# A gated linear-attention start-up rearranged: own gates for the last pair of heads, the next unit's decays moved into the MLP steps, other dummies between the transposes

## The chip, the cores and the metric

One core of a Trainium2 chip runs the whole program. The metric is the device time of one execution in microseconds (us), taken as the median of several runs. Runs of one kernel on one chip lie within about 0.7 % of each other here (the kernel before: 566.09 to 569.85 us on one chip). PE is TensorE (matmuls), PEld its weight loads, DVE is VectorE, ACT is ScalarE, POOL is GpSimd, SP is SyncE, which here only issues transfers.

## The reference, cut to what matters

An attention-like recurrence, then an MLP. `B, H, S, D = 4, 8, 768, 48`, model width 384, MLP width 2048.

```python
f = 1.0 / (1.0 + np.exp(-f_logit))
for t in range(S):
    state = f[:, :, t, :, None] * state + np.einsum('bhd,bhe->bhde', k[:, :, t], v[:, :, t])
    y[:, :, t] = np.einsum('bhd,bhde->bhe', q[:, :, t], state)
x = y.transpose(0, 2, 1, 3).reshape(B * S, H * D)
h = x @ w_in
g = np.where(h > 0.0, h, np.exp(np.minimum(h, 0.0)) - 1.0)
return g @ w_out
```

The weights arrive in 64-bit floating point, and the kernel makes 32-bit ones of them while the first unit's MLP runs.

## The kernel before

The tokens are worked through in 12 units of 256. A unit holds its 8 heads as 4 pairs: pairs 0 to 2 fill most of the partitions, and the last pair (number `NKT` = 3) sits in the same layout. For each pair, `gates` makes `1 + exp(-f_logit)` on ACT, `grow` makes its running product with a scan on DVE, `fall` takes the reciprocal of that (the decay itself), and `scale` multiplies k by the product and q by the reciprocal on POOL. In the kernel before, the last pair's gates are not computed for themselves. They are spread over the spare partitions of pairs 0 to 2, and two SBUF-to-SBUF transfers per unit (`move`, written f<-f in the traces) bring the results into place.

```python
def grow(u, p):
    g = qkf[u % NB]["f"][:, p, 0]
    nc.vector.tensor_tensor_scan(out=g, data0=g, data1=g, initial=1.0, op0=ALU.mult, op1=ALU.max)
def fall(u, p):
    f = qkf[u % NB]["f"]
    nc.vector.reciprocal(f[:, p, 1], f[:, p, 0])
def move(u, which, queue):
    f = qkf[u % NB]["f"]
    for r in range(2):
        to = PAD + D * r
        queue.dma_start(out=f[to : to + D, NKT, which], in_=f[GAP[r] : GAP[r] + PAD, 0:NKT, which])
```

Each of the 16 pieces of the weights passes four stations, in this order: `fetch` (a transfer, issued by SP), `split` (two DVE operations), `lower` (one ACT operation), `merge` (one DVE operation).

```python
def split(n):
    ...
    nc.vector.tensor_scalar(out=bits[:], in0=hi, scalar1=3, scalar2=0x3FFFFFF8,
        op0=ALU.logical_shift_left, op1=ALU.bitwise_and)
    nc.vector.tensor_scalar(out=hi, in0=hi, scalar1=-(2**30), scalar2=None, op0=ALU.bitwise_and)
def lower(n):
    ...
    nc.scalar.activation(raw.bitcast(U16)[:, 2::4], raw.bitcast(U32)[:, 0::2], AF.Copy, scale=2.0**-29)
def merge(n):
    ...
    nc.vector.tensor_tensor(out=to.bitcast(I32), in0=bits, in1=hi, op=ALU.add)
    fetch(n + AHEAD)
```

The first unit's MLP runs in 16 steps, alternately `up` (x times a piece of w_in) and, two pieces behind, `down` (times a piece of w_out). Work of the second unit is hung on these steps with `at_step(step, ...)`: `advance` (state sums on PE), `step` (the same on DVE), `scores` and `mask`, `outputs`, `carried` (which finishes x of the second unit and is followed by a move xt<-xt). `warm` issues dummy matmuls. In the traces of this case an engine's work stands in the order in which the program emits it: in c1 an elu of ACT whose product PE had finished at 29.8 ran at 35.76, behind an issue of ACT's own queue, 6.01 us idle before it. So the order of the lines below is the order of each engine's work.

```python
# start of the kernel before, cut
    ...                                     # first unit: three pairs, two moves, transposes, scores 0 to 2
    a = qkf[1]["f"][:, 0:NKT, 0]            # second unit, all before the first MLP step:
    nc.vector.tensor_scalar_add(a, a, 1.0)
    for p in range(NKT):
        grow(1, p)
    move(1, 0, nc.sync)
    ...
    fall(1, 0)
    ...
    mask(0, pc)
    ...
    split(0)
    ...
    fall(1, 1)
    first_outputs(0)
    lower(0); merge(0)                      # (two lines in the source)
    first_outputs(1)
    ...
    split(1)
    transposed(1, 0, "a0"); warm(1); transposed(1, 1, "a1")
    lower(1)
    watch(0)
    fall(1, 2)
    move(1, 1, nc.scalar)
    ...
    attention(1, (), A1)                    # A1 = (2, 4, 5, 7, 8, 9): steps of the second unit's parts
    for n in range(1, NFT):                 # merge 1 and later inside the steps
        ...
```

Of the kernel before, what the change touches and what calls it, by code (L numbers as in the profile page):

```python
# [356 lines left out]
def fast(ctx: ExitStack, tc: tile.TileContext, q, k, v, f_logit, w_in, w_out, out, flag, outer):  # L357
# [38 lines left out]
    WA = 1  # L396
    W0 = 3
    HOLD = 2
    A1 = (2, 4, 5, 7, 8, 9)
# [30 lines left out]
    def load(u, names="fkqv"):  # L430
        b, s0 = u // UPB, (u % UPB) * U
        for n in names.replace("v", ""):
            to = qkf[u % NB][n][MAIN]
            frm = src[n][b, :, :, s0 : s0 + U].rearrange("(p r) d s -> (r d) p s", r=2)
            if n == "f":
                to, frm = to[:, 0:NKT, 0], frm[:, 0:NKT]
            nc.sync.dma_start(out=to, in_=frm)
            for r in range(2 if n == "f" else 0):
                nc.sync.dma_start(
                    out=qkf[u % NB][n][GAP[r] : GAP[r] + PAD, 0:NKT, 0],  # L440
                    in_=src[n][b, 2 * NKT + r, :, s0 : s0 + U].rearrange("(i j) s -> i j s", i=PAD),
                )
        if "v" in names:
            nc.sync.dma_start(
                out=vs[u % NB][:, :, PAD : PAD + DM], in_=v[b, s0 : s0 + U].rearrange("(c t) n -> t c n", t=W)
            )
# [6 lines left out]
    def blank(i, *engines, zeros=None):  # L453
# [4 lines left out]
        (zeros or engines[-1]).memset(qkf[i]["f"][:, NKT], 1.0)  # L458
# [189 lines left out]
    def watch(u):  # L648
        nc.vector.scalar_tensor_tensor(
            out=fine[:], in0=qkf[u % NB]["f"][:, 0:NKT, 0, U - 1 :], scalar=LIMIT, in1=fine[:],  # L650
            op0=ALU.is_le, op1=ALU.mult,
        )
# [378 lines left out]
    def warm(n, bank="m0"):  # L1031

        pw = ps.tile([128, 4, 128], FP32, tag=bank, name="psW")
        for _ in range(n):
            nc.tensor.matmul(
                pw[:], lhsT=ident[:], rhs=ident[:].unsqueeze(1).broadcast_to([128, 4, 128]), start=True, stop=True
            )


    gates(0, (1, 2))  # L1040
# [5 lines left out]
    for p in range(NKT):  # L1046
        grow(0, p)
        scale(0, ("k", p, nc.gpsimd))
        if p < 2:
            transposed(0, 0, "m0", (p,))  # L1050
    move(0, 0, nc.scalar)
    transposed(0, 1, "m1", (0,))
    fall(0, 0)
    scale(0, ("q", 0, nc.gpsimd))
    warm(WA, "m3")
    gates(1, bias=0)
    advance(0, (0, 1))
    pc = scores(0, ("m2", "m3"), (0,))
# [5 lines left out]
    scale(0, ("k", NKT, nc.gpsimd), ("q", 1, nc.gpsimd))  # L1064
    fall(0, 2)
    move(0, 1, nc.scalar)
    warm(4)
    transposed(0, 1, "m1", (1,))
    advance(0, (2,))
    scores(0, None, (1,), pc)  # L1070
    scale(0, ("q", 2, nc.gpsimd))
    advance(0, (3,))
    scores(0, None, (2,), pc)
    nc.gpsimd.tensor_copy(
# [3 lines left out]
    a = qkf[1]["f"][:, 0:NKT, 0]  # L1078
    nc.vector.tensor_scalar_add(a, a, 1.0)
    for p in range(NKT):  # L1080
        grow(1, p)
    move(1, 0, nc.sync)
    scale(0, ("q", NKT, nc.gpsimd))
    warm(2)
    scores(0, None, (NKT,), pc)
    warm(1)
    fall(1, 0)
    for c in range(NC - 1):
        step(0, c)
    mask(0, pc)  # L1090
    step(0, NC - 1)
    split(0)
# [10 lines left out]
    fall(1, 1)  # L1103
    first_outputs(0)
    lower(0)
    merge(0)
    first_outputs(1)
    scale(1, ("k", 0, nc.gpsimd), ("q", 0, nc.gpsimd), ("k", 1, nc.gpsimd), ("k", 2, nc.gpsimd))
    scale(1, ("k", NKT, nc.gpsimd))
    split(1)  # L1110
    transposed(1, 0, "a0")
    warm(1)
    transposed(1, 1, "a1")
    lower(1)
    watch(0)
    scale(1, ("q", 1, nc.gpsimd))
    fall(1, 2)
    scale(1, ("q", 2, nc.gpsimd))
    move(1, 1, nc.scalar)
    watch(1)  # L1120
    at_step(1, lambda: scale(1, ("q", NKT, nc.gpsimd)))
    attention(1, (), A1)
    for n in range(1, NFT):
        t = min(max(needs[n][0] - 2, 0), n)
        at_step(t, lambda n=n: merge(n))
        if n > 1:
            later.setdefault(max(t - 2, 0), []).append(n)
    at_step(8, lambda: load(2))
# [90 lines left out]
```

## Time and profile before

The time before is 568.36 us, median of 3 runs (567.65 to 569.44). Its profiled run has a span of 565.7 us on the core.

| What | Kernel before |
| --- | --- |
| first ACT exp of the first unit | 4.84 us |
| score mask starts | 20.82 us |
| first MLP step starts | 30.80 us |
| third MLP step starts | 38.79 us |
| `carried` of the second unit | 56.65 us |
| second unit's first MLP product | 76.12 us |
| span | 565.7 us |

How to read it: from about 100 us on PE is full (460.0 us busy of the 460 from 100 to 560 us; 8.63 of 10 from 90 to 100), so the row that counts is the next to last. Whatever moves the second unit's first MLP product moves the end by about as much.

Beside the lines that the prediction shows, two more of the timeline of DVE are the second unit's second and third reciprocal in the kernel before; the columns are start, duration, engine and source line, operation, tiles and shapes.

```profile
24.12 1.75 DVE L630 RECIPROCAL f<-f 128x256 f32<-128x256 f32 x1
...
29.76 1.75 DVE L630 RECIPROCAL f<-f 128x256 f32<-128x256 f32 x1
```

A reciprocal of 128x256 took 1.69 to 1.76 us in this trace (36 of them, mean 1.75), a scan of that shape 0.66 to 1.16 (mean 0.77). The columns are the stretch, its length, then PE, weight loads, DVE, ACT and POOL, each with its number of instructions, then the granted clock, the DMA share and GB/s.

```profile
10.00:20.00 10.00, 9.24 (x132) 4.72 (x130) 8.31 (x10) 2.19 (x5) 5.12 (x10) 1.00 1.08 264
...
30.00:40.00 10.00, 8.68 (x100) 6.95 (x99) 7.51 (x12) 8.60 (x9) 1.47 (x2) 1.00 0.74 179
```

DVE is idle for 1.7 us of the first of these stretches, 2.8 of the one left out and 2.5 of the last, 7.0 of 30 us; in the two stretches after them, which the prediction shows, for under 1 us of 20.

### The profile page before, as it was taken

Reading aid. Unit: us, or ns where it says so; the run is one execution under the profiler, and the core shown is the slowest. Engines: PE = TensorE matmul, PEld = TensorE weight load, DVE = VectorE, ACT = ScalarE, POOL = GpSimd, SP = SyncE. Lnnn points to the kernel's source line nnn. Section 1 sums busy time; section 2 is a strip of 40 time slices with the busy share of each in tenths; the row PEclk is TensorE's granted clock in tenths of the full one; section 3 lists DMA queues with packets and bytes.
Section 4 is the critical chain, followed back from the end, with each engine's and each line's share of the span. In section 5 each row is a group of like instructions: output and inputs, shape, how many; then the busy total and the mean of one; then the engine's idle time right before and its main releaser. Section 6 shows DMA issues by size and latency. Waiting matters only on the chain.

```text
span 565.7 us, 15532 instructions
## 1 busy us (share of the span) xinstructions
PE 548.6 (97%) x6338; PEld 510.3 (90%) x6338; DVE 408.2 (72%) x802; ACT 230.6 (41%) x424; POOL 290.9 (51%) x567
## 2 busy tenths in 40 slices
PE   6898998999999999999999999999999999999996
PEld 3576777999999999999999999999999999999995
DVE  8689889785776785785785885886786876745543
ACT  3287953334343443433433343343334344233331
POOL 6510897474374374465466357257257348325332
PEclk9999999999999999999999999999999999999999
DMA  8989871023024135225216216216206202201001
GB/s 208 262 197 287 264 161 43 3 64 99 3 56 140 53 74 138 64 53 146 79 38 158 82 38 153 86 37 155 85 22 170 85 9 72 85 2 36 30 2 35
DMA packets 38193, 53.30 MB, mean 94 GB/s; under 512 B 3712, under 2 KB 27936, under 8 KB 38112
## 3 DMA queue, kind: packets, MB, share of 16 engines
q1 hardware_dynamic: 37312, 51.62, 34.6%
q8 instruction: 52, 0.85, 0.7%
q10 hardware_dynamic: 800, 0.59, 0.4%
q14 instruction: 29, 0.24, 0.2%
HBM read 44.04 MB, written 4.72 MB: 86 GB/s over the span
## 4 chain that ended last, share of the span: by engine, by line
PE 82%; DVE 6%; ACT 4%; DMA 4%; issue 2%; POOL 1%; SPq 0%; ACTq 0%; DVEq 0%; POOLq 0%
PE psH L881 37%; PE psM L980 36%; DMA area<-in_moe_w_in_dram 2%; ACT area L572 2%; PE psS L704 2%; PE psY L742 2%; PE psY L762 2%; PE psU_a L727 2%; DVE f L630 2%; PE psT L668 1%; DMA f<-f 1%; DVE f L625 1%; DVE bits L562 1%; DMA f<-in_f_logit_dram 0%; DVE area L566 0%
## 5 line engine op out<-in xcount | busy, mean ns | idle before, releaser
L881 PE MATMUL psH<-xt,wi 128*128 128x128 f32 (+1 forms) x1056 | 194.9, 293 | 0.0
L945 POOL TENSOR_TENSOR sums<-gg 128x128 f32<-128x128 f32 x176 | 77.5, 461 | 216.3 <-DVE gg L935 204.9
L881 PEld LDWEIGHTS psH<-xt,wi 128*128 128x128 f32 x1056 | 149.5, 192 | 1.4
L913 ACT ACTIVATE gg<-hh 128x512 f32<-128x512 f32 x88 | 55.6, 632 | 231.7 <-DVE hh L903 151.6
L881 PE MATMUL psH<-xt,area 128*128 128x128 f32 x704 | 121.8, 275 | 1.4 <-DVE gg L935 0.9
L881 PEld LDWEIGHTS psH<-xt,area 128*128 128x128 f32 x704 | 106.5, 191 | 6.4 <-DVE gg L935 1.0
L890 DVE TENSOR_TENSOR hh<-psH,u 128x256 f32<-128x256 f32 x88 | 37.2, 423 | 93.8 <-ACT u L888 93.8
L980 PE MATMUL psM<-area,sums 128*128 128x192 f32 x528 | 100.3, 326 | 0.0
L980 PEld LDWEIGHTS psM<-area,sums 128*128 128x128 f32 x528 | 88.2, 190 | 0.1
L980 PE MATMUL psM<-wo,gg 128*128 128x192 f32 x352 | 74.9, 335 | 0.0
L630 DVE RECIPROCAL f<-f 128x256 f32<-128x256 f32 x36 | 62.8, 1748 | 1.1
L935 DVE SCALAR_TENSOR_TENSOR gg<-gg,hh 128x512 f32<-128x512 f32 x88 | 61.9, 703 | 1.8 <-ACT gg L914 1.8
L914 ACT ACTIVATE gg<-gg 128x512 f32<-128x512 f32 x96 | 60.7, 632 | 3.0
L980 PEld LDWEIGHTS psM<-wo,gg 128*128 128x128 f32 x352 | 55.2, 190 | 2.0
L903 DVE TENSOR_TENSOR hh<-psH,u43h 128x256 f32<-128x256 f32 (+1 forms) x176 | 54.7, 353 | 3.0
L945 POOL TENSOR_TENSOR sums<-gg,sums 128x128 f32<-128x128 f32 x88 | 47.3, 538 | 6.9
L888 ACT COPY u<-psH 128x128 f32<-128x128 f32 x88 | 23.3, 264 | 60.3 <-PE psH L881 60.3
L903 DVE TENSOR_TENSOR u43h<-psH,hh 128x256 f32<-128x256 f32 x88 | 37.2, 423 | 12.4 <-PE psH L881 11.7
L620 POOL TENSOR_TENSOR k<-k,f 128x256 f32<-128x256 f32 x48 | 39.5, 824 | 8.2 <-DMA f<-f 5.1
L980 PE MATMUL psM<-area,gg 128*128 128x192 f32 x176 | 43.0, 326 | 0.0
L980 PE MATMUL psM<-wo,sums 128*128 128x192 f32 x176 | 43.0, 326 | 0.0
L945 POOL TENSOR_TENSOR sums<-sums,gg 128x128 f32<-128x128 f32 x88 | 42.8, 487 | 0.0
(97 smaller groups left out, 665.3 us busy)
## 6 DMA issues: line engine op xcount, KB each, us to landing
area<-in_moe_w_out_dram SPq DMA_DIRECT2D x8, 768.0 KB, 8.6
again<-in_moe_w_in_dram SPq DMA_DIRECT2D x16, 384.0 KB, 4.2
again<-in_moe_w_out_dram SPq DMA_DIRECT2D x16, 384.0 KB, 3.5
k<-in_k_dram SPq DMA_DIRECT2D x12, 384.0 KB, 4.6
q<-in_q_dram SPq DMA_DIRECT2D x12, 384.0 KB, 5.6
v<-in_v_dram SPq DMA_DIRECT2D x12, 384.0 KB, 6.1
area<-in_moe_w_in_dram SPq DMA_DIRECT2D x8, 576.0 KB, 8.8
out_dram<-o SPq DMA_DIRECT2D x42, 96.0 KB, 1.7
```

Of the source, the lines that this page charges most:

```text
L572: nc.scalar.activation(raw.bitcast(U16)[:, 2::4], raw.bitcast(U32)[:, 0::2], AF.Copy, scale=2.0**-29)
L620: e.tensor_tensor(out=t[n][:, p], in0=t[n][:, p], in1=t["f"][:, p, "kq".index(n)], op=ALU.mult)
L630: nc.vector.reciprocal(f[:, p, 1], f[:, p, 0])
L881: nc.tensor.matmul(to, lhsT=lhs, rhs=rhs, start=(n == 0), stop=True, skip_group_check=True)
L888: nc.scalar.copy(u1[:], pa[:, 0])
L890: add = lambda to, x, y: nc.vector.tensor_tensor(out=to, in0=x, in1=y, op=ALU.add)
L903: add = lambda to, x, y: nc.vector.tensor_tensor(out=to, in0=x, in1=y, op=ALU.add)
L913: nc.scalar.activation(g[:], h, AF.Relu, scale=-1.0)
L914: nc.scalar.activation(g[:], g[:], AF.Exp, scale=-1.0)
L935: nc.vector.scalar_tensor_tensor(out=g[:], in0=g[:], scalar=-1.0, in1=phs.pop(P), op0=ALU.add, op1=ALU.max)
L945: nc.gpsimd.tensor_tensor(out=s[:, i], in0=x, in1=y, op=op)
L980: nc.tensor.matmul(pm[bank][:, half * DH : (half + 1) * DH], lhsT=x, rhs=y, start=first, stop=(j == NP - 1), skip_group_check=True,)
```

## The change

The intent has three parts. First, the first unit's last pair gets gates, a scan and a reciprocal of its own, so that both moves of that unit go, and with them the late scores. Second, the second unit's decays (scans, reciprocals, scaling, transposes) leave the stretch before the first MLP step, so that the first unit's own path runs through unhindered; they are hung on the first unit's MLP steps. Its outputs and `carried` come three steps later as well. Third, the dummy matmuls between the transposes get other counts and lengths. The core of the diff:

```diff
-    A1 = (2, 4, 5, 7, 8, 9)
+    F1 = (0, 1, 3)
+    A1 = (3, 6, 7, 9, 11, 12)
@@ the first unit's f: one load, filled with 50 first
+            elif n == "f":
+                to = to[:, :, 0]
+            engines[-1].memset(qkf[i]["f"][:, :, 0], 50.0)
@@ the first unit
-    gates(0, (1, 2))
+    gates(0, (1, 1, 2))
-    for p in range(NKT):
+    for p in range(HP):
         grow(0, p)
         scale(0, ("k", p, nc.gpsimd))
-    move(0, 0, nc.scalar)
+        if p:
+            warm(1, "m3", 3)
...
     fall(0, 2)
-    move(0, 1, nc.scalar)
+    fall(0, 3)
@@ the second unit, before the MLP steps
-    for p in range(NKT):
-        grow(1, p)
-    move(1, 0, nc.sync)
-    fall(1, 0)
...
-    fall(1, 1)
-    fall(1, 2)
-    move(1, 1, nc.scalar)
+    grow(1, 0)
+    grow(1, 1)
+    merge(1)
+    grow(1, 2)
+    at_step(0, lambda: move(1, 0, nc.scalar))
     watch(0)
+    watch_last(0)
@@ and inside them
+    for p in range(NKT):
+        at_step(F1[p], lambda p=p: fall(1, p), lambda p=p: scale(1, ("q", p, nc.gpsimd)))
+    at_step(F1[2], lambda: move(1, 1, nc.scalar), lambda: watch(1))
+    at_step(A1[0], lambda: transposed(1, 0, "a0"), lambda: transposed(1, 1, "a1"))
```

(The order of `split(0)`, `lower(0)`, `mask(0)` and `split(1)` ahead of the steps changes a little too; left out here.)

More of the change, by code (lines that the diff above doesn't have):

```diff
@@ L395, in fast @@
     AHEAD = 7
-    WA = 1
+    F1 = (0, 1, 3)
     W0 = 3
     HOLD = 2
-    A1 = (2, 4, 5, 7, 8, 9)
+    A1 = (3, 6, 7, 9, 11, 12)
     D2 = (16, 18, 20, 22)
@@ L434, in load @@
             frm = src[n][b, :, :, s0 : s0 + U].rearrange("(p r) d s -> (r d) p s", r=2)
-            if n == "f":
+            if n == "f" and u:
                 to, frm = to[:, 0:NKT, 0], frm[:, 0:NKT]
+            elif n == "f":
+                to = to[:, :, 0]
             nc.sync.dma_start(out=to, in_=frm)
-            for r in range(2 if n == "f" else 0):
+            for r in range(2 if n == "f" and u else 0):
                 nc.sync.dma_start(
@@ L457, in blank @@
                 e.memset(qkf[i][n][:, j * w : (j + 1) * w], 0.0)
-        (zeros or engines[-1]).memset(qkf[i]["f"][:, NKT], 1.0)
+        if i:
+            (zeros or engines[-1]).memset(qkf[i]["f"][:, NKT], 1.0)
+        else:
+            engines[-1].memset(qkf[i]["f"][:, :, 0], 50.0)
     start = ctx.enter_context(ExitStack())
@@ L650, in watch, with watch_last @@
             out=fine[:], in0=qkf[u % NB]["f"][:, 0:NKT, 0, U - 1 :], scalar=LIMIT, in1=fine[:],
+            op0=ALU.is_le, op1=ALU.mult,
+        )
+    def watch_last(u):
+        nc.vector.scalar_tensor_tensor(
+            out=fine[:, 0:1], in0=qkf[u % NB]["f"][:, NKT:, 0, U - 1 :], scalar=LIMIT, in1=fine[:, 0:1],
             op0=ALU.is_le, op1=ALU.mult,
@@ L1029, in finish_flag, with warm @@
         nc.vector.tensor_copy(flag[:], pf[0:1, :])
-    def warm(n, bank="m0"):
+    def warm(n, bank="m0", blocks=4):
         pw = ps.tile([128, 4, 128], FP32, tag=bank, name="psW")
@@ L1035, in warm @@
             nc.tensor.matmul(
-                pw[:], lhsT=ident[:], rhs=ident[:].unsqueeze(1).broadcast_to([128, 4, 128]), start=True, stop=True
+                pw[:, 0:blocks], lhsT=ident[:], rhs=ident[:].unsqueeze(1).broadcast_to([128, blocks, 128]), start=True, stop=True
             )
-    gates(0, (1, 2))
+    gates(0, (1, 1, 2))
     fetch(0)
@@ L1045, in fast @@
     warm(W0, "m3")
-    for p in range(NKT):
+    for p in range(HP):
         grow(0, p)
         scale(0, ("k", p, nc.gpsimd))
-        if p < 2:
-            transposed(0, 0, "m0", (p,))
-    move(0, 0, nc.scalar)
-    transposed(0, 1, "m1", (0,))
+        if p:
+            warm(1, "m3", 3)
+        transposed(0, p // 2, f"m{p // 2}", (p % 2,))
     fall(0, 0)
     scale(0, ("q", 0, nc.gpsimd))
-    warm(WA, "m3")
-    gates(1, bias=0)
     advance(0, (0, 1))
+    warm(1, "m3")
     pc = scores(0, ("m2", "m3"), (0,))
@@ L1063, in fast @@
     fall(0, 1)
-    scale(0, ("k", NKT, nc.gpsimd), ("q", 1, nc.gpsimd))
+    scale(0, ("q", 1, nc.gpsimd))
     fall(0, 2)
-    move(0, 1, nc.scalar)
-    warm(4)
-    transposed(0, 1, "m1", (1,))
     advance(0, (2,))
+    warm(1)
     scores(0, None, (1,), pc)
     scale(0, ("q", 2, nc.gpsimd))
+    fall(0, 3)
     advance(0, (3,))
+    warm(1)
     scores(0, None, (2,), pc)
+    scale(0, ("q", NKT, nc.gpsimd))
     nc.gpsimd.tensor_copy(
@@ L1077, in fast @@
     )
-    a = qkf[1]["f"][:, 0:NKT, 0]
-    nc.vector.tensor_scalar_add(a, a, 1.0)
-    for p in range(NKT):
-        grow(1, p)
-    move(1, 0, nc.sync)
-    scale(0, ("q", NKT, nc.gpsimd))
-    warm(2)
+    warm(1)
     scores(0, None, (NKT,), pc)
     warm(1)
-    fall(1, 0)
+    gates(1, bias=0)
     for c in range(NC - 1):
         step(0, c)
+    split(0)
+    lower(0)
     mask(0, pc)
-    step(0, NC - 1)
-    split(0)
     for c in range(NC - 1):
@@ L1102, in fast @@
         fetch(n)
-    fall(1, 1)
+    merge(0)
+    step(0, NC - 1)
     first_outputs(0)
-    lower(0)
-    merge(0)
+    split(1)
     first_outputs(1)
-    scale(1, ("k", 0, nc.gpsimd), ("q", 0, nc.gpsimd), ("k", 1, nc.gpsimd), ("k", 2, nc.gpsimd))
-    scale(1, ("k", NKT, nc.gpsimd))
-    split(1)
-    transposed(1, 0, "a0")
+    lower(1)
     warm(1)
-    transposed(1, 1, "a1")
-    lower(1)
-    watch(0)
-    scale(1, ("q", 1, nc.gpsimd))
-    fall(1, 2)
-    scale(1, ("q", 2, nc.gpsimd))
-    move(1, 1, nc.scalar)
-    watch(1)
-    at_step(1, lambda: scale(1, ("q", NKT, nc.gpsimd)))
-    attention(1, (), A1)
+    a = qkf[1]["f"][:, 0:NKT, 0]
+    nc.vector.tensor_scalar_add(a, a, 1.0)
+    grow(1, 0)
[3 more added lines that the diff above has]
+    at_step(0, lambda: move(1, 0, nc.scalar))
+    watch(0)
+    watch_last(0)
+    scale(1, ("k", 0, nc.gpsimd), ("k", 1, nc.gpsimd), ("k", 2, nc.gpsimd))
     for n in range(1, NFT):
         t = min(max(needs[n][0] - 2, 0), n)
-        at_step(t, lambda n=n: merge(n))
+        if n > 1:
+            at_step(t, lambda n=n: merge(n))
         if n > 1:
             later.setdefault(max(t - 2, 0), []).append(n)
+    for p in range(NKT):
+        at_step(F1[p], lambda p=p: fall(1, p), lambda p=p: scale(1, ("q", p, nc.gpsimd)))
+    at_step(F1[1], lambda: scale(1, ("k", NKT, nc.gpsimd)))
+    at_step(F1[2], lambda: move(1, 1, nc.scalar), lambda: watch(1))
+    at_step(F1[2] + 3, lambda: scale(1, ("q", NKT, nc.gpsimd)))
+    at_step(A1[0], lambda: transposed(1, 0, "a0"), lambda: transposed(1, 1, "a1"))
+    attention(1, (), A1)
     at_step(8, lambda: load(2))
```

## The prediction

> **What bounds the kernel now.** I read the page first (engine shares and the strip of 40 slices), then the busy time of each engine by stretches, then the chain of waits, then the timeline of the first 100 us line by line.
>
> ```profile
> PE 548.6 (97%) x6338; PEld 510.3 (90%) x6338; DVE 408.2 (72%) x802; ACT 230.6 (41%) x424; POOL 290.9 (51%) x567
> ...
> 40.00:50.00 10.00, 10.00 (x99) 7.31 (x98) 9.42 (x17) 8.11 (x7) 0.00 (x0) 1.00 1.05 287
> 50.00:60.00 10.00, 8.28 (x150) 5.93 (x149) 9.72 (x17) 8.85 (x11) 1.31 (x3) 1.00 1.05 263
> ...
> 200.00:250.00 50.00, 50.00 (x581) 48.67 (x581) 37.75 (x76) 20.25 (x42) 26.66 (x51) 1.00 0.33 88
> ```
>
> The columns after the stretch are its length, then PE, weight loads, DVE, ACT, POOL, granted clock, DMA share and GB/s. From about 100 us on PE is full to the end. So the change, which touches only the first two units, can move the end only by moving the moment at which PE becomes full. Between 40 and 60 us DVE is at 9.4 and 9.7 of 10: that stage is DVE and PE in near balance.
>
> The timeline of the start, which the change rewrites:
>
> ```profile
> 0.80 0.40 SPq L437 DMA_DIRECT2D f<-in_f_logit_dram  x1
> 1.73 0.98 POOL L458 MEMSET f<- 128x512 f32 x2
> 4.84 0.42 ACT L611 ACTIVATE f<-f 128x256 f32<-128x256 f32 x1 [2.75 <-DMA f<-in_f_logit_dram]
> 8.61 4.94 DVE L630 RECIPROCAL f<-f 128x256 f32<-128x256 f32 x3
> 15.43 1.07 POOL L620 TENSOR_TENSOR k<-k,f 128x256 f32<-128x256 f32 x1 [3.12 <-DMA f<-f]
> 18.85 0.72 POOL L620 TENSOR_TENSOR q<-q,f 128x256 f32<-128x256 f32 x1 [0.60 <-DMA f<-f]
> 20.82 1.29 DVE L712 TENSOR_TENSOR at<-psS,twice 128x512 f32<-128x512 f32 x2 [1.74 <-PE psS L704]
> 24.73 0.66 PE L807 MATMUL psY<-at,padded_v 64*32 64x64 f32 x33 [1.34 <-issue]
> 28.48 0.48 ACT L817 COPY xt<-psY 128x384 f32<-128x384 f32 x1 [0.77 <-PE psY L807]
> 30.80 2.76 PE L926 MATMUL psH<-xt,wi 128*128 128x256 f32 x12
> 33.45 0.96 DVE L580 CUSTOM_DVE_ANT_0 wi<-area,bits 128x1536 uint16<-128x1536 uint16 x1 [1.93 <-ACT area L572]
> 34.55 2.83 PE L926 MATMUL psH<-xt,wi 128*128 128x256 f32 x12 [0.99 <-DVE wi L580]
> ```
>
> The reader is to see four things. The first f load is issued at 0.80, waiting for nothing. The last pair's k and q wait for the two SBUF moves (f<-f): k at 15.43, q at 18.85. The score mask starts at 20.82, only because those scores were late. The MLP starts at 30.80, and its second step waits for a weight that DVE has to merge. After 30.80 the remaining idle of PE, up to the point where it is full, is small: 1.0 at 33.6, 0.3 at 38.5, 1.35 at 50.7, 0.3 at 52.3, 0.8 at 77.2, 0.5 at 93.4, 0.9 at 96.3, about 5.2 us in all. With the start itself this is all there is to win.
>
> [...]PE is mostly idle from 22.8 to 25.9, and the stretches 26 to 30 show granted clocks 0.66, 0.50, 0.50, 0.63. [...]
>
> **The change part by part.**
>
> (1) First load of f: one transfer of 384 KB in place of 288 and two of 48 KB, but the whole of f is first filled with 50 by POOL. That memset is POOL's third, from 1.73; 1024 elements at the row's 0.49 per 512 are 0.98, so it ends at 2.71 and the load is issued at 2.75 instead of 0.80. I take 3.6 us to landing (288 KB took 3.3; all 384 KB took 3.9 with the gaps apart): 6.35. ACT starts at 6.45 against 4.84, so **1.6 later**.
>
> (2) Gates in pieces 1, 1, 2. Exp and +1 of 0.42 each, 0.6 for two pairs: scans can start at 7.35, 8.1, 9.35, 10.1 and end at 10.9. DVE then makes four reciprocals of 1.65 (a fourth scan and a fourth reciprocal are new work, 2.4 us): 17.5. POOL's last q product 0.72, then scores 0.45: 18.75, against 20.69 before (20.23 plus 0.46). Removed: both moves, 5.1 and 5.4 us from issue to use. The PE queue with its short dummies (0.65 for three blocks, 0.86 for four, from 0.43 a record) is ready at 18.2, so it does not bind. **Net 1.9 earlier.**
>
> (3) DVE then makes two state sums and the first weight split (1.15, now ahead of the mask): mask from 19.4 to 20.7, against 20.82 to 22.1. **1.4 earlier.** From mask end to x written took 22.1 to 29.94 in the old trace (3.3 first outputs with the 1.34 gap, 0.4, 2.6, 1.46); taken over unchanged, x is there at 28.5. The second unit's transposes and dummies, which held PE until 30.80, are out of the way. So the MLP starts at 28.6: **2.2 earlier.**
>
> (4) What was paid for it. The second unit's three scans, one addition and three reciprocals were done before the MLP in DVE time in which little waited for it. Now the third scan and reciprocals stand between weight merges. ACT's lowering of weight 1 comes behind the x copies: 28.5 to 30.5, DVE having nothing from about 26.2 on, some 4 us of idle. Merge 1: 30.5 to 31.5. Then scan 0.6, watch 0.25, reciprocal 1.7, split 1.15, reciprocal 1.7, split 1.15: 38.05, then the elu 0.65 and merge 2 (0.98): 39.65. Before, merge 2 ended at 38.65. So the third MLP step starts at 39.7 against 38.79: the 2.2 are gone, **0.9 lost** instead.
>
> (5) The rest of the first unit. DVE needs per step a merge 0.98, a split 1.15 and half an elu 0.33: 2.46. PE needs 2.59 (step starts 65.78, 68.37, 70.95, 73.54). DVE therefore catches up only 0.13 a step, and has the third reciprocal (1.75), sums (2.1) and mask (1.2) on top. PE has advance, scores, outputs and carried (1.15, 1.16, 1.5, 1.35). Following both queues in program order: up2 39.7, down0 42.3, up3 46.35 (waits for merge 4), down1 49.0, up4 51.6, scores 54.2, down2 55.35, up5 58.25 (merge 8), outputs 61.6 (mask), down3 63.0, carried 65.6, up6 66.95, down4, up7, down5 at 69.55, 72.15, 74.75, and the second unit at 77.3. Before: 76.12. **1.2 later.**
>
> (6) The second unit's x comes out three steps later (step 12 instead of 9). Carried ends at 66.95, ACT copies after its pending lowering 69.6 to 71.5, the move took 6.0 before: 77.5, and POOL's blend needs three of its five operations (3.79 for five, so 2.3) for the second product. If the move is as slow again, **0 to 2.3 more**; the blend had 3 us to spare before (done at 73.34).
>
> The sum: plus 1.2 to plus 3.5, less what (3) may be better than I took it.
>
> **The rivals.** First, the early gain survives: if the 1.34 us instruction gap and the half clock (36 small products in 1.17 and 1.49 us) do not recur, x is 1 to 2 us earlier still, merge 1 with it, and DVE's debt is cancelled: minus 1 to minus 2.5, 566 to 567.5. For it: the step numbers look tuned to the new order. Against: DVE was full from 37.5 to 62.5 and gets 2.4 us more work. Second, DVE becomes the bound of the first unit's steps, as worked out: 569.5. Third, x of the second unit arrives too late, POOL is held at the blend, and as it is 8 to 9 tenths busy from 60 to 100 us its backlog delays the sums too: 571 to 573. Fourth, PE idles from about 35 to 39.7 and drops to half clock: 1.3 to 2.6 more in the third step, but hidden where DVE binds.
>
> **Range and chances.** Second and third rival are plus 1.2 to plus 4, the first minus 1 to minus 2.5; I give the first 4 in 10, as small timing shifts decide it. Weighted: about plus 0.6. Predicted 569.0 us against 568.36, range 565.5 to 572.5. Two per cent is 11.4 us, more than the 5.2 us of idle plus the start shift could give, so faster 0.02, within 0.95, slower 0.03.
>
> **What would show it.** (1) f issue near 2.75 and first ACT exp near 6.4. (2) no f<-f on the first unit; last scores near 18.7. (3) first MLP product at 28 to 29. (4) DVE idle of some 4 us before merge 1, and the third MLP step at 39 to 40 waiting for DVE. (5) the second unit's first product at 77 or later, DVE over 9 tenths from 31 to 62. (6) a wait of PE or POOL for xt<-xt near 77. It is wrong if the second unit starts before 75.5, if ACT starts its exp before 5.5, or if PE shows new gaps after 100 us.

## The result, and the profile after

| | before | after |
| --- | --- | --- |
| time, median (same rounds, 4 runs each) | 568.66 us | 572.16 us |
| range | 567.65 to 569.44 | 571.24 to 572.57 |
| first ACT exp | 4.84 | 6.66 |
| last scores of the first unit | 20.23 | 19.81 |
| score mask starts | 20.82 | 20.39 |
| first MLP step starts | 30.80 | 27.13 |
| third MLP step starts | 38.79 | 39.37 |
| `carried` of the second unit | 56.65 | 67.90 |
| second unit's first MLP product | 76.12 | 79.62 |
| span of the profiled run | 565.7 | 569.4 |

The result is correct. The ratio is 1.0060, 95 % interval 1.0039 to 1.0082. Here and below a ratio is the mean time of one kernel's fast runs over that of the other's of the same rounds, so it is not quite the ratio of the medians quoted. The changed kernel is 0.6 % slower, inside 2 % and inside the predicted range, but at its upper end: 3.5 us lost where 0.6 was predicted. (On the chip of the experiments below the same kernel loses 4.9 to 5.1 us by its ratio of 1.0087.)

The line numbers in the trace after are 5 to 11 higher than before; it is the same code. The start, from the timeline of ACT, DVE and PE of the changed kernel:

```profile
6.66 0.42 ACT L616 ACTIVATE f<-f 128x256 f32<-128x256 f32 x1 [4.57 <-DMA f<-in_f_logit_dram]
11.26 6.56 DVE L635 RECIPROCAL f<-f 128x256 f32<-128x256 f32 x4
20.39 1.29 DVE L723 TENSOR_TENSOR at<-psS,twice 128x512 f32<-128x512 f32 x2 [0.63 <-PE psS L715]
27.13 2.86 PE L937 MATMUL psH<-xt,wi 128*128 128x256 f32 x12 [0.49 <-ACT xt L830]
29.07 0.96 DVE L585 CUSTOM_DVE_ANT_0 wi<-area,bits 128x1536 uint16<-128x1536 uint16 x1 [1.73 <-ACT area L577]
```

The reader is to see that the intent came true. The first step starts 3.67 us earlier than before, the second step 4.37 us earlier (30.18 against 34.55). Then it is lost. The same view, from DVE's and PE's timeline, for the next ten microseconds:

```profile
30.72 0.73 DVE L660 SCALAR_TENSOR_TENSOR fine<-f,fine 128x1 f32<-128x1 f32 x1
31.38 1.74 DVE L635 RECIPROCAL f<-f 128x256 f32<-128x256 f32 x1
...
33.56 0.96 DVE L571 TENSOR_SCALAR area<-area 128x768 int32<-128x768 int32 x1
34.44 1.74 DVE L635 RECIPROCAL f<-f 128x256 f32<-128x256 f32 x1
...
38.10 1.12 DVE L585 CUSTOM_DVE_ANT_0 wi<-area,bits 128x1536 uint16<-128x1536 uint16 x1
...
41.20 1.75 DVE L635 RECIPROCAL f<-f 128x256 f32<-128x256 f32 x1
...
38.46 0.69 PE L679 MATMUL psT<-ident,k 128*128 128x128 f32 x2 [4.80 <-POOL k L625]
39.37 5.37 PE L937 MATMUL psH<-xt,wi 128*128 128x256 f32 x12 [0.22 <-DVE wi L585]
```

Two reciprocals stand between merge 1 (29.07) and merge 2 (38.10), and a third follows at 41.20. PE meanwhile waits 4.80 us for the last pair of the second unit's k, which waits for a move, and when it has that, the third step's weight is only just merged. Two chains, one over DVE and one over the move and POOL, end within a microsecond of each other, at 39.2 and 38.4. And the third step itself takes 5.37 us against 2.83: PE runs at half clock (granted clock 0.50 from 38 to 44 us). The stretches, with the granted clock third from the end:

```profile
30.00:40.00 10.00, 4.80 (x22) 3.78 (x23) 9.83 (x14) 5.50 (x5) 3.28 (x4) 0.88 0.78 199
40.00:50.00 10.00, 10.00 (x92) 7.48 (x91) 9.65 (x14) 8.17 (x9) 0.98 (x1) 0.77 0.90 242
...
60.00:70.00 10.00, 8.79 (x153) 6.51 (x152) 9.83 (x14) 8.23 (x8) 9.06 (x13) 1.00 1.05 322
```

From 30 to 70 us DVE is at 9.3 to 9.8 of 10 (9.32 in the stretch left out), and PE has 5.2 us of idle in the first of these stretches alone. Before, PE was at 8.68 there. The last loss comes at the end of the second unit's attention, from the timeline of ACT and PE:

```profile
65.89 1.94 ACT L577 ACTIVATE area<-area 128x768 uint16<-128x768 uint32 x1
67.57 0.47 ACT L760 COPY between<-psY 128x8 f32<-128x8 f32 x2
...
67.90 1.35 PE L773 MATMUL psY<-q,state 64*64 64x64 f32 x64 [1.21 <-ACT between L760]
...
79.62 0.38 PE L892 MATMUL psH<-xt,wi 128*128 128x128 f32 x2
```

PE waits for two small copies of ACT, which stand in ACT's queue behind a weight's lowering, and that waits for DVE's split, which ended at 65.9. After 79.62 the two traces run side by side to the end, 3.5 us apart at the start and 3.7 at the end.

### The profile page after: what moved, and what is told of

Its sections match the earlier page's. It is cut to its first block, busy times and chain, and to the rows that moved or that the text cites. A ratio compares the mean times of both kernels' runs of the same rounds, so it can differ in the third digit from the quotient of the medians.

```text
span 569.4 us, 15523 instructions
## 1 busy us (share of the span) xinstructions
PE 549.0 (96%) x6338; PEld 510.0 (90%) x6338; DVE 413.3 (73%) x805; ACT 231.0 (41%) x426; POOL 294.1 (52%) x567
## 4 chain that ended last, share of the span: by engine, by line
PE 83%; DVE 5%; ACT 3%; DMA 2%; issue 1%; POOL 1%; ACTq 0%; SPq 0%; DVEq 0%
PE psH L892 37%; PE psM L991 36%; ACT area L577 2%; PE psS L715 2%; PE psY L753 2%; PE psY L773 2%; PE psU_a L738 2%; DMA area<-in_moe_w_in_dram 2%; PE psT L679 1%; DVE f L635 1%; PE psM L969 1%; DVE bits L567 1%; DVE wi L585 1%; DVE wo L585 1%; DVE gg L946 1%
## 5 line engine op out<-in xcount | busy, mean ns | idle before, releaser
L635 DVE RECIPROCAL f<-f 128x256 f32<-128x256 f32 x37 | 64.4, 1746 | 1.1
L625 POOL TENSOR_TENSOR q<-q,f 128x256 f32<-128x256 f32 x48 | 36.4, 758 | 18.1 <-DMA f<-f 6.8
```

What stands on the lines that cost most here:

```text
L625: e.tensor_tensor(out=t[n][:, p], in0=t[n][:, p], in1=t["f"][:, p, "kq".index(n)], op=ALU.mult)
```

## The experiments

All twelve but one give the reference's result; that one is wrong. The times of before that the ratios of the twelve use are of the same chip (567.2 to 567.4 us; 568.66 for the result itself, on another chip). This table has what each run's profile says of the two points that matter. The profile is of one execution: the same kernel gave 79.62 (after) and 80.60 (after_again), so differences of under 1 us in its columns are not resolved.

| run | second unit's first product | span | span less product | median | ratio to before (95 %) |
| --- | --- | --- | --- | --- | --- |
| before | 76.12 | 565.7 | 489.6 | 568.36 | |
| after | 79.62 | 569.4 | 489.8 | 572.16 | 1.0060 (1.0039 to 1.0082) |
| k1_keep_clock | 80.14 | 570.5 | 490.4 | 572.30 | 1.0089 (1.0062 to 1.0116) |
| k2_cheap_recip (wrong result) | 77.55 | 567.0 | 489.5 | 569.92 | 1.0050 (1.0022 to 1.0078) |
| k3_first_only | 88.51 | 577.7 | 489.2 | 580.26 | 1.0232 (1.0204 to 1.0261) |
| k4_second_only | 80.82 | 570.8 | 490.0 | 572.41 | 1.0085 (1.0057 to 1.0113) |
| after_again | 80.60 | 570.7 | 490.1 | 572.35 | 1.0087 (1.0066 to 1.0107) |
| k3b_first_only | 77.41 | 566.9 | 489.5 | 568.54 | 1.0026 (0.9999 to 1.0052) |
| r3_early | 81.15 | 570.4 | 489.3 | 571.88 | 1.0087 (1.0059 to 1.0114) |
| r4_early_pool | 81.85 | 570.1 | 488.3 | 573.49 | 1.0109 (1.0080 to 1.0139) |
| c1_order | 79.12 | 568.6 | 489.5 | 571.09 | 1.0078 (1.0056 to 1.0100) |
| c2_all | 77.41 | 567.2 | 489.8 | 569.53 | 1.0042 (1.0025 to 1.0060) |
| d1_late_fall | 76.98 | 566.2 | 489.2 | 568.72 | 1.0016 (0.9997 to 1.0036) |
| e1_best | 78.54 | 566.8 | 488.3 | 567.54 | 0.9994 (0.9976 to 1.0013) |

The theories on the table after the result were three. A: DVE's queue is the bound from 29 to 67 us; the second unit's third scan and three reciprocals, now between the merges, cost what is lost. B: the half clock in the third step costs it. C: the second unit's x comes three steps later and is late.

C was already weak from the trace after. POOL's blend of the second unit's x does wait for the late move, but PE, one product later, waits for a DVE result and not for the blend:

```profile
77.22 3.19 POOL L880 TENSOR_TENSOR xt<-xt 128x128 f32<-128x128 f32 x5 [4.31 <-DMA xt<-xt]
...
81.06 0.71 PE L892 MATMUL psH<-xt,area 128*128 128x128 f32 x4 [0.39 <-DVE gg L946]
```

Before, the wait at the same place was 0.86 us. The column "span less product" says the same: with the late x (after, after_again, k1, k2, k4, r3, r4) it is 488.3 to 490.4, with the early x (before, k3, k3b, c1, c2, d1) 489.2 to 489.8, and with e1's, one step later than the early one, 488.3.

**k1_keep_clock: take the half clock away.** Five dummy matmuls in the gap before the late transposes keep PE busy.

```diff
+    at_step(A1[0], lambda: warm(5))
     at_step(A1[0], lambda: transposed(1, 0, "a0"), lambda: transposed(1, 1, "a1"))
```

> Five dummies fill PE's idle before the second unit's transposes, so that the third MLP step runs at full clock (about 2.8 us in place of 5.4). Theory A (DVE, and ACT behind it, set the first unit's steps): DVE's work is untouched, the product 'carried' still waits for ACT's copy near 67.6, the second unit starts within 0.8 us of 79.6, time 571.4 to 572.3. Theory B (the half clock of the third step is the loss): everything after it comes 2.3 to 2.6 us earlier, time 569.5 to 570.

The third step is at full speed now, from PE's timeline, and nothing is gained:

```profile
40.24 2.76 PE L937 MATMUL psH<-xt,wi 128*128 128x256 f32 x12
...
68.41 1.35 PE L773 MATMUL psY<-q,state 64*64 64x64 f32 x64 [1.84 <-ACT between L760]
```

2.6 us are saved in the third step (2.76 against 5.37; granted clock 1.00 from 30 to 50 us). The step starts 0.9 later (the dummies had ended at 37.56; the transposes waited 1.74 us more for POOL's product of the last pair's k, which ended at 39.91 in this execution against 38.41), is 1.4 ahead at the next `up` (46.94 against 48.33), and has given it all back at `carried`: 0.5 later than in the trace after, with the wait for ACT grown from 1.21 to 1.84, and 0.6 us of new waits at the scores, of which the later 0.21 names DVE's state. So the half clock was hidden behind DVE in the changed kernel. B falls for it; in kernels in which DVE no longer binds it comes back, as k2 and e1 show below.

**k2_cheap_recip: take the reciprocals' duration away.** The second unit's three reciprocals become memsets, 0.27 us each in place of 1.74. The result is wrong (relative error 335); every other instruction, wait and transfer stays.

```diff
-        at_step(F1[p], lambda p=p: fall(1, p), ...
+        at_step(F1[p], lambda p=p: nc.vector.memset(qkf[1]["f"][:, p, 1], 1e-12), ...
```

> Wrong result on purpose: the second unit's three reciprocals inside the MLP steps are replaced by memsets of that tile (about 0.3 us each instead of 1.7), so DVE has some 4.2 us less to do between 31 and 43 us. Theory A (DVE bound): merges, mask and ACT's copies come 3 to 4 us earlier, second unit starts at 76 to 77, time 568 to 569.3. Theory B (half clock): the second unit's last k still waits for the move that lands near 37, PE still idles 4 us and drops to half clock, gain under 1 us: 571.2 to 572. Theory C (the second unit's x is late because its steps were put later): gain at most 1 us.

It ran 2.2 us faster than k1 in the same rounds (0.39 % by the two ratios), and its second unit starts 2.1 us earlier than after. That is about half of the 4.4 us taken away (three times 1.74 less 0.27). The rest is not A's: PE's timeline shows the next bound at once.

```profile
39.57 0.69 PE L679 MATMUL psT<-ident,k 128*128 128x128 f32 x2 [6.08 <-POOL k L625]
40.05 4.09 PE L937 MATMUL psH<-xt,wi 128*128 128x256 f32 x12
```

Merge 2 starts at 35.17 now instead of 38.10, but PE waits 6.08 us for the last pair's k, whose decays come by the move. From 40.05 to 77.55 PE is then without a gap. With the wait the half clock is back as well (granted clock 0.80 from 30 to 40 us, 0.86 from 40 to 50): the third step takes 4.09 us against 2.83, and as PE has no gap afterwards, these 1.3 us count here; they are most of the 1.4 that remain to before's 76.12. So A holds as far as it goes: DVE's queue is the longest chain, and the move with the late transposes is a second one, which lets the third step start no earlier (40.05 against 39.37).

**k4_second_only and k3_first_only: one part of the change alone.** For k4 the kernel before gets only the second part (F1, A1, the new order of the second unit's work and of the first weights' conversion), for k3 only the first unit's new gates, with the second unit's decays before merge 1 as they were.

```diff
 k4, on the kernel before:
-    A1 = (2, 4, 5, 7, 8, 9)
+    F1 = (0, 1, 3)
+    A1 = (3, 6, 7, 9, 11, 12)
-    ... grow(1, p), move(1, 0), fall(1, 0), fall(1, 1), fall(1, 2) before the steps
+    ... as in the change, without watch_last
```

```diff
 k3, on the changed kernel:
-    A1 = (3, 6, 7, 9, 11, 12)
+    A1 = (2, 4, 5, 7, 8, 9)
-    ... merge(1) between the scans, fall(1, p) at the steps F1
+    for p in range(NKT):
+        grow(1, p)
+    move(1, 0, nc.sync)
+    split(1)
+    fall(1, 0)
+    ... fall(1, 1), fall(1, 2), then merge(1); transposes after the first step
```

> Only the second unit's part: first unit as before with its moves and three-pair gates, second unit's decays and transposes inside the MLP steps at the new step numbers. Theory A: the DVE time between 13.5 and 20.8 that before used for the second unit now lies idle, while 6 us of work come into the full stretch: MLP starts near 29.5, second unit near 81, 573 to 575.5. Rival (the first unit's fourth pair and its later load are the cost): 568 to 570.

> Only the first unit's part of the change: own gates for the last pair, no moves; the second unit's scans and reciprocals all before the second weight's merge, and its attention at the steps of before (transposes at step 2). Theory A: DVE does the same sum of work, wins only the 1.7 us it idled before merge 1, and starts the MLP's second step near 33; 570 to 571.5. Rival (placing the decays inside the steps is the whole cost): 566.5 to 568.

k4 alone costs as much as the whole change: 1.0085. Its busy time by stretches shows why, against the lines of before further above.

```profile
10.00:20.00 10.00, 9.01 (x130) 4.69 (x130) 4.92 (x7) 1.89 (x5) 4.18 (x7) 1.00 1.11 250
...
30.00:40.00 10.00, 5.04 (x26) 3.94 (x24) 9.27 (x12) 5.32 (x5) 3.60 (x4) 0.92 0.76 192
```

DVE falls from 8.31 to 4.92 between 10 and 20 us, where it has room, and rises from 7.51 to 9.27 between 30 and 40, where it has none. The first MLP step does start 2.1 us earlier (28.70), and none of it is left by the third (40.97 against 38.79). There PE had waited 5.27 us for POOL's product of the last pair's k (it ended at 40.43, merge 2 at 39.84), so both chains of the changed kernel are in k4 too; `carried` at 69.10 waits 1.37 us for ACT's copies again.

k3 was spoiled by its own construction and says nothing of the first part. The move stood on SP's queue behind weight fetches, one of which (31.31, 8.37 long) was held by a wait of 7.2 us for the unit's second move f<-f, which ACT had issued at 33.27 (the two share a semaphore), so the first move was issued at 40.40 and PE's transposes waited 14.62 us:

```profile
46.63 0.69 PE L679 MATMUL psT<-ident,k 128*128 128x128 f32 x2 [14.62 <-POOL k L625]
```

**after_again and k3b_first_only: a control, and the first part alone built anew.** k3b has the move on ACT's queue.

```diff
-    move(1, 0, nc.sync)
     split(1)
     fall(1, 0)
     first_outputs(1)
+    move(1, 0, nc.scalar)
     lower(1)
```

> The changed kernel unaltered, as a control on the chip of the next three. Every theory: 3 to 4 us above before, ratio 1.005 to 1.008, carried near 67.9 us, second unit near 79.6.

> First part of the change alone, built anew: the first unit's four pairs with their own gates and no moves, but all decays of the second unit made by VectorE before merge 1, the move on ScalarE's queue, x moved out at the old steps. The theory that VectorE's order decides: the decays sit before merge 1 again, so merge 1 comes near 33, but none stands between merges later: merge 2 by 37 to 38.5, second unit's first product 75 to 77, time within 1.5 us of before. The theory that the late x decides (the second part's later steps for moving x out, not VectorE): the second unit's products near 76 as well, but then the run with the second part and early transposes would not come down either. Rival, that the first part itself costs (later f load, four separate gates): 570 to 572.

The control repeats the result at 1.0087. The first part alone is at 1.0026, with the second unit at 77.41: 3.2 us earlier than the control, 1.3 later than before. From its DVE and PE timeline:

```profile
33.10 0.94 DVE L585 CUSTOM_DVE_ANT_0 wi<-area,bits 128x1536 uint16<-128x1536 uint16 x1
...
34.68 0.69 PE L679 MATMUL psT<-ident,k 128*128 128x128 f32 x2 [2.70 <-POOL k L625]
```

Merge 1 is at 33.10 as expected, and merge 2 at 38.16. So the four kernels can be set side by side: neither part 76.12, first alone 77.41, second alone 80.82, both 79.62 and 80.60. The second part costs 2.2 to 4.7 us, the first costs 1.3 alone and nothing, or less, beside the second. (k3b's transposes stand after the first step, not before it as in before, so it is not the first part to the letter.) The loss is the second part's.

**r3_early and r4_early_pool: mend it by moving less.** r3 puts the third scan, the move and the first reciprocal ahead of merge 1 and the second pair of transposes two steps later. r4 also gives merges 3, 5 and 7 to POOL.

```diff
-    merge(1)
     grow(1, 2)
-    at_step(0, lambda: move(1, 0, nc.scalar))
+    move(1, 0, nc.scalar)
+    fall(1, 0)
+    merge(1)
...
-    at_step(A1[0], lambda: transposed(1, 0, "a0"), lambda: transposed(1, 1, "a1"))
+    at_step(A1[0], lambda: transposed(1, 0, "a0"))
+    at_step(A1[0] + 2, lambda: transposed(1, 1, "a1"))
 r4 also:
-            at_step(t, lambda n=n: merge(n))
+            at_step(t, lambda n=n: merge(n, nc.gpsimd if n in (3, 5, 7) else None))
```

> The changed kernel with the second unit's third scan, its move and its first reciprocal ahead of merge 1, and the second pair of transposes two steps later. If VectorE's total between 29 and 67 us decides, moving 2.4 us of it ahead of merge 1 delays merge 1 by about 2.4 us (to 31.5) but the work between there and carried is the same: second unit 79 to 80, time as the changed kernel within 1 us. If PE's stall at the late transposes (4.8 us before 38.46) decides, it is gone here: second unit at 77 to 78, 1.5 to 2.5 us below the changed kernel.

> As the run before it, with merges 3, 5 and 7 on GpSimd in place of VectorE: 2.9 us less on VectorE between 39 and 67 us. If VectorE decides: carried 2 to 3 us earlier than in the run before it, second unit 76.5 to 77.5, time 2 to 3 us below it. If GpSimd's work slows VectorE as much as it relieves it, or GpSimd's own backlog holds the merges: no gain or 1 to 2 us lost.

r3 is level with the control (571.88 and 572.35), as theory A said of it. The 4.8 us stall at the late transposes is gone, and PE waits elsewhere instead: 3.27 us for merge 2 at 37.94, and then, because the late transposes' copies stand behind two lowerings in ACT's queue, 2.92 us before the state sums.

r4 is a miss, and the more useful one. Three merges fewer on DVE gained nothing. From DVE's timeline:

```profile
38.60 2.08 DVE L571 TENSOR_SCALAR area<-area 128x768 int32<-128x768 int32 x1
```

The split that runs beside a POOL merge (38.19 to 40.27) takes 2.08 us instead of 0.56, and later, at 48.22, DVE waits 1.73 us for POOL's merge. Beside POOL's work these DVE operations were slower, and the traces show for how long: in r4 the operation ended 0.41 us after POOL's (40.27 for the merge, 40.68 for the split; 53.83 and 54.25 the second time), and in the trace after, beside POOL's products of q, the splits' second operation took 0.96 us in place of 0.56 and ended 0.42 after them (34.10 and 34.52, 37.17 and 37.59). So in these four cases the DVE operation lasted until POOL's was over, however short it is alone.

**c1_order, c2_all, d1_late_fall, e1_best: keep the first part, and order the queues.** Each of these starts from k3b and adds to the one before it. c1 moves merge 1 ahead of the second and third reciprocal.

```diff
-    fall(1, 1)
-    scale(1, ("k", NKT, nc.gpsimd))
     watch(0)
     watch_last(0)
+    merge(1)
+    fall(1, 1)
+    scale(1, ("k", NKT, nc.gpsimd))
...
-    at_step(2, lambda: transposed(1, 0, "a0"), lambda: transposed(1, 1, "a1"))
+    at_step(3, lambda: transposed(1, 0, "a0"), lambda: transposed(1, 1, "a1"))
     A1: (2, 4, 5, 7, 8, 9) becomes (3, 5, 6, 7, 8, 9)
```

> The first part alone again (as the kernel that came out near before), with merge 1 moved from behind the second unit's three reciprocals to behind the first of them, the transposes after the second step and the sums one step later. VectorE has the same work. If the order of VectorE's queue decides: merge 1 at 30 instead of 33.1, the third step's weight merged by 37.5 to 38, second unit's first product 75 to 76.5 instead of 77.4, time 1 to 2 us below the first part alone, so level with before. If VectorE's total decides and the order does not: second unit at 77.4 and no gain.

A miss: 1.0078. Merge 1 came at 29.78, as expected, but merge 2 ended at 39.81 instead of 37.5 to 38. ACT's timeline has the reason:

```profile
34.49 1.22 ACTq L642 DMA_DIRECT2D f<-f  x2
35.76 0.60 ACT L924 ACTIVATE gg<-psH 128x512 f32<-128x512 f32 x1 [6.01 <-PE psT L679]
```

ACT stands still for 6.01 us. The name in brackets misleads here, because those transposes had been done at 35.0; what ACT waited for is the line above it, the issue of the second move on ACT's own queue (34.49). That waits for DVE's third reciprocal (done at 34.46), and ACT's elu of the first step (PE was done at 29.8) and the lowering of weight 2 stand behind it. So the wait of an issue was a wait of the queue that makes it, here for 6.01 us. PE had a gap of 4.92 us meanwhile, and its third step took 5.46 us at half clock (granted clock 0.71 from 40 to 50 us).

c2 adds two things that shorten DVE's and the first unit's path: POOL fills f first, so that the f load is issued earlier (at 1.78; 2.71 in the changed kernel), and ACT makes the +1 of the second unit's gates.

```diff
+        if not i:
+            engines[-1].memset(qkf[i]["f"][:, :, 0], 50.0)      # ahead of the fills of k and q
-        else:
-            engines[-1].memset(qkf[i]["f"][:, :, 0], 50.0)
...
-    gates(1, bias=0)
+    gates(1)
-    nc.vector.tensor_scalar_add(a, a, 1.0)
```

> As the run before it, with two things more: GpSimd's fill of the first f tile comes first in its queue, so the f load is issued near 1.8 us instead of 2.7, and the +1 of the second unit's gates is made by ScalarE, which takes 0.7 us off VectorE ahead of the scans. If VectorE is the bound from 10 us on, both come out whole: last scores near 19.0, merge 1 near 28.5, second unit 1.2 to 1.7 us earlier than in the run before it (73.5 to 75), time 1 to 2.5 us below before, the one version that would beat both. If a transfer of the weights or the move of the decays takes over as the bound: less than 0.7 us gained.

The ratio falls from 1.0078 to 1.0042, the second unit comes 1.7 us earlier, as expected; it does not get below before, as ACT's 6 us stall is still in it. d1 takes that away: the third reciprocal goes behind merge 2, the second move two steps later.

```diff
-    fall(1, 2)
-    scale(1, ("q", 2, nc.gpsimd))
-    move(1, 1, nc.scalar)
-    watch(1)
+    at_step(2, lambda: fall(1, 2), lambda: scale(1, ("q", 2, nc.gpsimd)), lambda: watch(1))
+    at_step(3, lambda: move(1, 1, nc.scalar))
```

> As the run with all three edits, where ScalarE stood still for 6 us because the second move of the decays was issued on its queue and waited for VectorE's third reciprocal, so that the first step's elu and the third weight came late. Here the third reciprocal stands behind merge 2 and the move two steps later. If the order in VectorE's and ScalarE's queues decides: merge 2 ends near 35.5 instead of 38.4, third step at 35.5, second unit's first product 74 to 76 instead of 77.4, time 1.5 to 3 us below the run before it, 0.5 to 1.5 below before. If VectorE's total decides: second unit at 77 again, no gain.

Merge 2 is at 34.44 and the third step at 35.68, three microseconds ahead of before (38.79), as expected. Of these, little reaches the second unit's product (76.98 against 77.41 in k3b and c2, less than two profiles of one kernel differ), from PE's timeline:

```profile
35.68 2.83 PE L937 MATMUL psH<-xt,wi 128*128 128x256 f32 x12 [1.16 <-DVE wi L585]
41.12 0.31 PE L738 MATMUL psU_a<-v,kn 64*64 64x48 f32 x2 [2.61 <-ACT kn L683]
```

ACT's copies of the transposed k stand behind the lowering of a weight, whose split stands behind the third reciprocal. After this gap of 2.61 us PE ran at half clock (granted clock 0.83 from 40 to 50 us): the sums and the next `down` took 5.59 us against 3.89 at full clock, and there is no gap after them in which the 1.7 us could be made up. e1 issues the transposes and their copies ahead of that lowering, and `outputs` and `carried` one step later.

```diff
             up(P)
+            if T == 2:
+                transposed(1, 0, "a0")
+                transposed(1, 1, "a1")
     A1: (3, 5, 6, 7, 8, 9) becomes (3, 5, 6, 7, 9, 10)
```

> As the run before it, where the state sums waited 2.6 us for ScalarE's copies of the transposed k, which stood behind the lowering of weight 4, and that behind VectorE's third reciprocal. Here the transposes and their copies are issued right after the second MLP step, ahead of that lowering; outputs and carried come one step later, so that the mask has time. If these queue positions are what is left: sums right behind the third step (38.5 instead of 41.1), third step still at 35.7, second unit's first product 74 to 75.5 instead of 77.0, time 1 to 2.5 us below the run before it and 0.5 to 2 below before, which would beat both kernels. If VectorE's total decides by now, the mask and merges stay where they are: second unit within 0.7 us of 77.0, no gain.

The sums follow the third step without a gap (38.71), as expected, and the time is level with before: 567.54 us, ratio 0.9994 with an interval that holds 1. It is the best version of the first part and well below the changed kernel, but it does not beat before. Its profiled run was the slowest of its six (568.87; the fastest was 566.46), and its second unit is late because of something new, from PE's timeline:

```profile
46.65 1.76 DVE L696 TENSOR_TENSOR state<-psU_a,state 128x192 f32<-128x192 f32 x4
...
48.05 2.49 PE L715 MATMUL psS<-q,k 64*64 64x64 f32 x64 [2.66 <-issue]
50.47 4.97 PE L969 MATMUL psM<-wo,gg 128*128 128x384 f32 x8
```

PE, done with `up` at 45.4, does nothing for 2.66 us, and then it runs at half clock to 54.8 (granted clock 0.50 from 48 to 54 us, 0.60 from 54 to 55). The view names no releaser for the gap, but the trace has a likely one. The scores write the PSUM tiles from which DVE's four state sums read. The four ran from 46.65 to 48.41, so by equal shares the third ended near 47.97, and the first score product ran at 48.05; from 48.53, after the last of them, the scores' weight loads ran on. PE's own part of the sums was ready at 39.86, but DVE came to them only at 46.65, behind merges, splits and an elu of its queue. So it is most likely DVE's order once more; no run moved the sums, and whether the gap is in e1's other runs is open. DVE is at 9.4 of 10 from 30 to 60 us in e1 too; how much a better order would still gain is not shown.

One thing the runs c1 to e1 have in common was not tried. In each of them a wait of PE of 2.6 us or more inside the steps (4.92 us in c1 and c2, 2.61 in d1, 2.66 in e1) was followed by a few microseconds at half clock, and PE has no gap from there to the second unit's product (c2 one of 0.61), so they count. Against the same steps at full clock it is 2.6 us in c1, 1.7 in c2 and d1, and 3.4 in e1 (the scores 2.49 against 1.16, the `down` 4.97 against 2.85). No run put k1's dummies into those gaps. If nothing else then binds, d1 and e1 would have their second unit near 75.3 and 75.1, before the 76.12 of before; that is an estimate from these differences, not a result.

## Why the prediction was right or wrong

The class and the range were right. The point was 3.2 us too low, and three of its six steps (2, 3 and 5) were off in size.

- Step 1, the f load 1.6 later: right. Issued at 2.71 (predicted 2.75), ACT's exp at 6.66 (6.45), so 1.8 later than before.
- Step 2, last scores 1.9 earlier: the sign was right, the size was not. They start at 19.81, so they end at 20.27 against 20.69: 0.4 earlier. The four reciprocals end at 17.8 and POOL's last product at 18.6, near the predicted 17.5 and 18.2. But the step said that PE's queue with its dummies "is ready at 18.2, so it does not bind", and it was not: the third pair's scores ran at 18.36, then a dummy (two records, 1.13 us, where 0.86 was taken), and the last scores only behind that, some 1.1 us late. The change did not add this: the kernel before has a longer one there (18.32, four records, 1.98 us), and there too the dummy and not q (done at 19.57) kept the last scores until 20.23, which the prediction's reading of the trace left out. No run took it away. The mask, at 20.39, was 0.4 earlier instead of 1.4.
- Step 3, MLP 2.2 earlier at 28.6: undersized, for a good reason. It started at 27.13, 3.67 earlier, although the mask was later than predicted. The step took over the 1.34 us gap and the half clock of the kernel before "unchanged". Neither recurred: the two groups of 36 small products took 0.91 and 0.86 us where they had taken 1.17 and 1.49 (granted clock 1.00 from 20 to 30 us, 0.83 before). The first rival had named exactly this.
- Step 4, the reciprocals between the merges: right in mechanism, with two terms off that cancel. Merge 1 started 1.4 earlier than predicted (29.07 against 30.5), DVE having been idle for 1.73 us and not 4. But the stretch from merge 1's end to merge 2's start took 8.15 us instead of 7.17: the two watches 0.83 against 0.25, the two splits 1.40 each against 1.15, both slowed beside POOL. Third step at 39.37, predicted 39.7.
- Step 5, "carried 65.6", second unit at 77.3: this is the step that failed. Up to the mask DVE kept its predicted time (it ended at 61.4; the step's 61.6). But the outputs started at 62.75, and `carried` at 67.90. The wait that set this is one that the step left out: `carried` needs two copies of ACT, and these stand behind the lowering of a weight that waits for DVE's split, which ended at 65.9. PE's own queue was late too, by 1.1 us at the outputs (no gap from 39.37 to 66.7, the half clock in it), but that was hidden behind the copies: k1, without the half clock, has its outputs at 62.35 and `carried` no earlier, at 68.41. So the missing term is the wait for the copies, 2.3 us. From `carried` to the second unit it took 11.7 us, as predicted.
- Step 6, late x, 0 to 2.3 more: 0, as the lower end said.

So the second rival was the right mechanism and too small by 2.3 us; the third had the right size for the wrong reason. The fourth was right in both halves, the half clock came and k1 shows it hidden. What was wrong in the weighing was the first rival: its condition came true and its consequence did not. An earlier start was worth nothing, because the chain behind it was bound by DVE's queue, and the third step came later than before all the same. Given 4 chances in 10, it drew the point from about plus 2.6 (the middle of the other two) to plus 0.6; the middles, weighed as the text says, give plus 0.9. Smaller still: the second move took 5.3 us from issue to use (13.58 to 18.85), not 5.4.

What is shown: the loss is the second part's (k4), in the changed kernel it is not the half clock (k1), and the duration of the three reciprocals is about 2.2 us of it (k2), of 3.5 in the result's call or 4.9 to 5.1 in the experiments'. What is argued only: that the rest is the second chain over the move and the late transposes, with the half clock that its wait brings (1.3 us in k2); no run took away both at once. That the move lands 7 us after its issue is in the trace (30.71 to 37.67). Its first packet moved only at 35.38 and its last ended at 37.02, and from 33 to 36 us the DMA engines were full with packets of the weights (share 1.00 to 1.07), so it probably queued behind them; no run tested that.

## What to carry to other kernels

An engine that is a quarter idle before a stage and 95 % busy inside it should do its odd work before: count the busy time of each engine by stretches first, and move work only from full stretches to empty ones. When an in-order queue carries both long waits (a transfer's issue or a lowering that waits for another engine) and short copies that a third engine needs, look for the copy behind the wait; it was the wait that the prediction missed, and it spoiled r3, c1 and d1 as well. An early gain counts only as far as the next engine that has no idle time. And look at the clock after each wait of PE: here waits from 2.6 us on (d1, e1) were followed by up to 3.4 us more at half clock (e1), which cost nothing where DVE bound the stage (k1) and counted in full where PE had no gap afterwards (k2).

## What the traces show of the clock and of issues, and what stays open

- The granted clock fell to 0.50 after waits of PE of different length. In e1 PE stopped at 45.39, and the clock is at 1.00 from 46 to 47 us, at 0.98 from 47 to 48 and at 0.50 from 48 on, so it fell close to 48, about 2.6 us later; in the changed kernel it fell at 37.70, 4.0 us after PE had stopped at 33.67; in d1 the gap before it was 2.61 us. In the kernel before it fell at 26.32, with PE busy for 1.30 of the 3.10 us from 22.8 to 25.9. The half clock lasted 3.4 us in the kernel before (26.32 to 29.74) and 6.8 us in the changed kernel (37.70 to 44.52) and in e1 (from about 48 to 54.8). What decides between the two lengths was not tested.
- Issues of transfers waited for another queue's transfer with which they share no data. In the changed kernel two issues of weight fetches on SP waited for a move f<-f that ACT had issued, 8.9 and 8.7 us; in the kernel before one did, 8.1 us. The trace shows why: the waiting issues carry the same semaphores as the moves (103 in the kernel before: the move issued at 31.58, the fetch at 36.78), so this is the program's choice of semaphores. k3 shows what it cost the work behind such an issue: 14.62 us of PE.
- Nothing in the profile explains the gap of 1.34 us in the kernel before (ahead of 24.73), in which PE waits for nothing that it shows; the changed kernel has no gap of that size at that place.
